# Two more tiles' skip term moved from TensorE to VectorE, with x's rows kept in the spare half of a small tile

## The chip, the cores and the metric

One Trainium2 chip, one of its cores. The time is that of one execution on the device in microseconds (us), as the median of several; lower is better. The engines are named as the profile names them: PE (TensorE, matrix products; PEld is its loading of weights), DVE (VectorE), ACT (ScalarE), POOL (GpSimd) and SP (SyncE, which here only issues transfers).

## The reference

Input x has 2048 rows (positions) of 512 channels. Two branches are computed from it and mixed by a gate per row. In the kernel's types all is bf16 outside, with sums in fp32.

```python
g = sigmoid((x * gate_w).sum(-1, keepdims=True))
# branch a: a diagonal complex recurrence over the 2048 positions, with a skip term
Bu = einsum("bld,pd->blp", x, B_bar)
for t in range(L):
    h = Lam_bar * h + Bu[:, t, :]
a = 2.0 * einsum("blp,dp->bld", hseq, Cmat).real + x * Dskip
# branch b: linear attention, 32 heads of 16; features are softmax(p) and softmax(-p)
phi_q, phi_k = features(q @ w_phi), features(k @ w_phi)
o = (phi_q @ (phi_k^T v)) / (phi_q . sum(phi_k) + 1e-6)
b = o @ wo
out = g * a + (1 - g) * b
```

The change is about `x * Dskip`, the skip term.

## The kernel before

The 2048 positions are sorted by their residue modulo 8, so that the recurrence can be run on blocks of eight positions; a tile is 128 positions of one residue, and there are 16 tiles. The output stage takes them in the order of the list `order`; "tile n" below is the n-th of that list.

**How the order of the work is set.** Each piece of work is a Python generator, `st_...`, that issues a few instructions for one engine and yields. The string `ORDER` (lines 24 to 53) lists some 850 tokens, and line 983's loop calls one generator for each. A token is a stage's name with, after `@`, the PSUM banks (of eight) that it uses, and after `:D` the wish that its copy or scaling be done by DVE rather than by ACT. The tile framework adds the semaphore waits. So the order on every engine's queue, and the choice between ACT and DVE, are written out by hand or by a planner outside the kernel; each engine works its queue strictly in order.

**The stages.** Names that matter below:

- `Z`: products of a tile of zeros with itself, the first thing on PE (line 324). The tile is `warm`.
- `Lk`, `Lx`, `Lb`, `Lc`, `Lq`, `Lv`, `Lo`, `Ld`: loads from HBM on SP's queue. `Ld` (line 260) loads the row of `Dskip` and some of x's rows.
- `k0..15`, `v0..15`, `q0..15`: products that give keys, values and queries of a tile, and their evacuation from PSUM by ACT or DVE (lines 505 to 526).
- `x`, `n`, `e`, `s` with a digit, and `X`, `N`, `E`, `S` for the four query groups of four tiles each: maximum, minimum, exponential and normalisation of the features (lines 550 to 614). `E` is two ACT instructions of 2048 elements per partition (line 567). `S` ends with a scaling on DVE (line 609) and a transpose by DMA into `phT` (line 613).
- `a0..4`: sums over the keys.
- `b`, `g`, `l`, `c`, `z`, `H`, `h`, `p`: the recurrence, with scalings by ACT (line 444) or DVE (line 446), sums on DVE and sums by POOL's DMA (line 529).
- `y`: a tile's products of the states with C (line 875); then, for a tile that is not in the list `XD`, the skip term as four products of x's transposed block with a diagonal matrix of `Dskip` (line 882), into the same PSUM bank.
- `o`: products of the query features with the key sums (line 894) into a pair of banks, logarithm and exponential on ACT (lines 898, 901), a multiplication on DVE into `on` (line 907). `O` transposes `on` by DMA (line 930).
- `t`: products with `wo`, added into y's bank (line 943), and the multiplication by the gate out of PSUM: by ACT (line 949) or DVE (line 951), or for a tile in `XD` by one DVE instruction that also adds the tile `xd` (line 947).
- `u`: for a tile in `XD`, one DVE instruction that makes `xd` = x's rows times the gate times `Dskip` (line 913).
- `R`: the store.

Before the change `XD` has tiles 8 to 11. Their x rows lie in the space of the tile `WKV` that the folded key weights leave when the last `k` stage is done; `xl` returns a tile's rows.

Of the kernel before, what the change touches and what calls it, by code (L numbers as in the profile page):

```python
# [24 lines left out]
B:D Lk Lk Z@0 Lx Z Z Z Z Z Z W00@1 Z B B B W01@2 W01 W01:D W00 W00 W10@0 Lx W11@3 Lx T0@4 B W11 T0 f1@2 Lx Lx f0@1 f0  # L25
W10:D f1:D T1@5 T1:D f2@3 f2 f3@0 f3:D k0@6 x0z:D Lx k1@7 V@3 V P U U k1 k1 k0 k0 P k3@3 P2 P P2 U P2 U k6@2 P2 P2 x0
Lx Lb Lx Lb P4 n0 P4 k3 x0 V2@6 P4 V2 P3 i3 gw P2 n0 P3 k5@7 x0 i3 x0 Lc k5 k9@3 k9 i0 Ld k2@0 M n0 i3 i3 k10@1 i3
k4@3 i0 M k2 i0 i0 i0 M Lb k10 i2 M k6 n0 k4 k7@0 k7 i2 Lb k8@7 i1 i2 x0 i1 i1 k13@6 M2 k11@0 n0 i2 k8 i1 x1 n1 x1 D
n1 x1 b200@1 i2 i1 L i0:D x1 D c1:D n1 Lc Lc i3:D n1 k11 e0 b010@7 b010 c0:D x1 n1 i2:D b200 x2 s0 c0:D s0 k12@3 k12
x2 g200@2 g200 n2 c1 b100@0 s0 b100 x2 b001@5 n2 Lv b000@7 Lc i1 b000 b111@4 b111 x2 n2 s0 n2 g000@2 b001 s0 c3:D  # L30
b011@3 b101@7 e1 x2 n2 g000 g000 Lx g001@5 g001 x3 s1 v1@4 b011 c3 s0 c2:D c2:D c1:D k14@2 g010@3 g010 Lo e2 x3 n3 s1
k13 D v0@0 v1 s1 g011@1 x3 c3:D g011 x3 g001 g011 v0 e2 k15@0 g011 g010 c0:D Lq Lq g010 s1 n3 k14 w2@6 c3 s0 D k15 n3
a0@54 s2 a0 g011 x3 n3 g011 Ld g010 g201@2 b101 Ld n3 s1 w2 g010 z0 b201@1 b201 z0 b110@7 n4 s1 x4 g101@3 g201 l2:D s2
s2 x4 n4 e3 z0 z0 w1@6 w1 b110 g100@2 g100 g101 g101 g100 s2 s2 s2 g111@1 l2:D l2:D g111 n4 g110@0 g110 e3 g110 g111
v2@2 v3@3 x4 n4 g110 g111 g111 g110 l2:D z0 v2 z0 v3 w3@2 s1 z0 g111 s3 g110 w0@7 w3 a1 a1 x4 c1 g301@6 z0 z1 z1 x4 w0
c2 g301 s3 g300@2 g300 z0 q3@7 q3 n4 e4 v5@6 z0 s2 s2 q2@2 s3 e4 q0@7 q0 z1 z1 l2:D z1 H0:D z1 s3 z1 z1 s4 v4@3 v4 q2
q1@0 H0 z1 v7@1 q1 X0 s3 q7@7 q7 z1 s4 N0 X0 v6@3 b300@0 N0 H0 b301@7 H0:D H0 N0 X0 v6 N0 s3 a2 v5 a2 c0 a2 v7 a2 X0
b301 s3 b300 q4@1 l3:D l3:D l3 c2 X0 N0 H1 H1:D H1:D q4 s4 q5@0 l3 q5 q6@7 g210@6 q6 X1 N1 h0:D H1:D E0 b211@0 X1 s4
E0 b210@7 X1 s3 b210 b311@1 b310@3 g211@2 s4 N1 S0 b211 N1 S0 s4 s4 l3:D X1 g311@7 N1 s4 g210 g210 b310 g211 g211 H1
g310@3 h0 h0 h0 g210 h1:D g211 g210 h1 b311 g211 g210 h0 g211 z2 z2 S0 z2 z2 z2 z2 g311 h1 g311 g311 h1 g310 g310 g310  # L40
S0 p00 v9@2 z2 g310 g310 g311 g311 v8@6 v15@1 S0 z2 z3 v10@7 p00 v12@3 v9 v8 S0 S0 v15 v11@6 z3 z2 z2 H2 v10 q11@2
p00:D z3 z3 z3 H2 a3 a3 H2 v12 z3 H2 H2 v11 h2 p10:D z3 z3 S0 z3 a3 a3 z3 p01 X1 h1 H3 q8@3 H3 H3 q10@6 q10 v14@7 h2
h2 H3 H3 v13@1 v13 p00:D S0 h2 q11 a4 v14 N1 q9@6 h2 q9 h3:D h3:D q12@1 a4 q8 h3 q12 X2 p10 E1 E1 a4 a4 Y S0 h3 h3 Y
X2 G q13@3 q13 G Y Y y1@1 y0@0 y0 N2 END p01 y0 o0@6 p00 p11 o0 S1 o1@4 o1 q15@2 o0 p10 p10 X2 y3@3 S0 y1 p11 S1 o0 X2
# [978 lines left out]
```

## Time and profile before

| | us |
|---|---|
| median of 3 runs | 149.02 (148.68 to 149.03) |
| the profiled execution | 148.95 |
| its span, first to last instruction | 147.2 |
| PE busy in the span | 140.8 |
| DVE busy | 135.1 |
| ACT busy | 123.4 |
| POOL busy | 45.4 |

The span is the time between the first and the last instruction of the profiled execution; what is left of its time lies around it. Busy time is the sum of the instructions' durations with overlaps counted once. Consecutive matrix products overlap in the pipeline, so a product's recorded duration is longer than the distance to the next one; distances are read from the chain or the timeline. The chain of waits starts at the last instruction and goes back at each step to what released it. In a timeline, a bracket holds the idle time in front of an instruction and what ended it. The line numbers in the rows are those of the kernel before. The granted TensorE clock was 1.00.

### The profile page before, as it was taken

The numbers are of one execution on the slowest core, as the hardware profiler recorded it, in microseconds if no ns is written. First come the engines' busy times: TensorE is split into PE (matmuls) and PEld (weight loads), VectorE is DVE, ScalarE is ACT, GpSimd is POOL, SyncE is SP. The second block draws the span as 40 slices with busy tenths as digits, with TensorE's granted clock in tenths as the row PEclk, the third lists the DMA queues.
The fourth block names the chain that finished last, engine by engine and source line by source line (L and its number), as shares of the span: only waits on it lengthen the run. The fifth ranks groups of instructions, "written<-read, shape, count | busy, mean of one in ns | idle before, by whom it ended". The sixth has DMA issues, their size and how long they took to land.

```text
span 147.2 us, 2881 instructions
## 1 busy us (share of the span) xinstructions
PE 140.8 (96%) x1014; PEld 73.3 (50%) x1014; DVE 135.1 (92%) x330; ACT 123.4 (84%) x222; POOL 45.4 (31%) x61
## 2 busy tenths in 40 slices
PE   6999999999999999999999999999979999999990
PEld 2744444444544644554454656545445554545650
DVE  2879999999999999999999999999998999979740
ACT  3479999999999999999999999999988997912110
POOL 7503600003138195797545353051003003000000
PEclk9999999999999999999999999999999999999999
DMA  5999998990846586789878969969988999999643
GB/s 123 233 184 170 181 179 160 239 290 2 195 94 90 88 114 99 80 127 169 131 111 141 144 90 191 123 126 164 208 179 153 192 214 159 199 180 271 129 111 114
DMA packets 56047, 22.63 MB, mean 154 GB/s; under 512 B 44768, under 2 KB 54880, under 8 KB 56032
## 3 DMA queue, kind: packets, MB, share of 16 engines
q1 hardware_dynamic: 47584, 15.05, 52.7%
q0 software_dynamic: 7504, 7.09, 33.8%
q10 hardware_dynamic: 944, 0.31, 0.9%
q8 instruction: 8, 0.13, 0.4%
q14 instruction: 7, 0.06, 0.1%
HBM read 2.51 MB, written 2.10 MB: 31 GB/s over the span
## 4 chain that ended last, share of the span: by engine, by line
DVE 45%; PE 36%; ACT 9%; DMA 4%; issue 3%; DVEq 0%
PE PS L875 17%; PE PS L943 8%; DVE EE L597 6%; DVE mn L544 5%; DVE mx L544 5%; DMA phT<-EE 4%; DVE EE L555 4%; DVE sq L575 4%; DVE EE L561 3%; PE PS L894 3%; PE PS L493 3%; PE PS L324 2%; DVE w L723 2%; ACT vx L137 2%; ACT Xq L137 2%
## 5 line engine op out<-in xcount | busy, mean ns | idle before, releaser
L567 ACT ACTIVATE EE<-EE 128x2048 bf16<-128x2048 bf16 x16 | 30.3, 1933 | 0.4 <-DVE EE L561 0.4
L493 PE MATMUL PS<-WKV,xT 128*128 128x480 bf16 (+1 forms) x128 | 29.2, 372 | 0.2 <-ACT WKV L137 0.2
L493 PEld LDWEIGHTS <-xT 128*128 128x128 bf16 x192 | 18.1, 97 | 19.7 <-issue 0.9
L137 ACT CAST Xq<-PS 128x480 bf16<-128x480 f32 x32 | 17.5, 592 | 0.2
L653 PE MATMUL PS<-xT,BT 128*128 128x512 bf16 x64 | 16.2, 379 | 0.0
L875 PE MATMUL PS<-C,H 128*128 128x512 bf16 x64 | 15.6, 379 | 0.0
L943 PE MATMUL PS<-Wo,oT 128*128 128x512 bf16 (+2 forms) x68 | 15.5, 366 | 0.0
L493 PE MATMUL PS<-Wq,xT 128*128 128x480 bf16 x64 | 14.9, 365 | 0.0
L641 PE MATMUL PS<-xT,BT 128*128 128x512 bf16 x64 | 14.8, 379 | 0.0
L529 POOL DMA_DIRECT2D C<-CT x4 | 6.8, 1712 | 18.1 <-DVE CT L446 18.1
L907 DVE TENSOR_TENSOR on<-PS,rd 128x512 bf16<-128x512 f32 x16 | 10.9, 684 | 1.0 <-ACT rd L901 0.9
L529 POOL DMA_DIRECT2D eb<-dg x4 | 4.8, 1201 | 22.3 <-ACT dg L444 10.9
L949 ACT ACTIVATE ot<-PS,G 128x512 bf16<-128x512 f32 (+1 forms) x10 | 6.3, 647 | 4.7 <-PE PS L943 4.7
L641 PEld LDWEIGHTS <-BT 128*128 128x128 bf16 x64 | 6.3, 98 | 7.5
L561 DVE TENSOR_TENSOR EE<-mn,Xq 128x2048 bf16<-128x2048 bf16 (+1 forms) x9 | 9.9, 1095 | 0.0
L555 DVE TENSOR_TENSOR EE<-Xq,mx 128x2048 bf16<-128x2048 bf16 (+1 forms) x9 | 9.8, 1094 | 0.0
L575 DVE TENSOR_TENSOR sq<-EE 128x2048 bf16<-128x2048 bf16 (+1 forms) x9 | 9.8, 1094 | 0.0
L943 PEld LDWEIGHTS <-oT 128*128 128x128 bf16 x68 | 6.4, 98 | 6.7
L898 ACT ACTIVATE ld<-PS 128x32 f32<-128x32 f32 x16 | 3.0, 202 | 7.8 <-PE PS L894 7.8
L597 DVE TENSOR_TENSOR EE<-EE,rc 128x2048 bf16<-128x2048 bf16 x8 | 9.6, 1210 | 0.0
L653 PEld LDWEIGHTS <-BT 128*128 128x128 bf16 x64 | 6.1, 97 | 6.9 <-issue 0.2
L137 ACT CAST vx<-PS 128x512 bf16<-128x512 f32 x16 | 9.5, 618 | 0.0
(196 smaller groups left out, 329.7 us busy)
## 6 DMA issues: line engine op xcount, KB each, us to landing
out_dram<-ot SPq DMA_DIRECT2D x7, 256.0 KB, 2.5
C<-CT POOLq DMA_DIRECT2D x4, 256.0 KB, 5.2
eb<-CT POOLq DMA_DIRECT2D x4, 256.0 KB, 4.3
eb<-dg POOLq DMA_DIRECT2D x4, 256.0 KB, 4.3
sq<-sq POOLq DMA_DIRECT2D x3, 256.0 KB, 3.8
WKV<-in_B_wqkv_dram SPq DMA_DIRECT2D x1, 512.0 KB, 4.9
Wo<-in_B_wo_dram SPq DMA_DIRECT2D x1, 512.0 KB, 4.1
WKV<-in_A_x_dram SPq DMA_DIRECT2D x2, 256.0 KB, 4.8
```

The source lines that it names most:

```text
L137: nc.scalar.copy(out=out_ap, in_=in_ap)
L493: MM(out=pt[:], lhsT=xT[:, kt, ti * P:(ti + 1) * P], rhs=W[:, kt, :], start=(kt == 0), stop=(kt == KT - 1))
L544: VT(out=dst, in0=cur[:, :, :, 0:n, :], in1=cur[:, :, :, n:2 * n, :], op=op)
L555: VT(out=half(EE, 0), in0=X5, in1=live["mx", p].to_broadcast([P, L, 8, Dh, 4]), op=ALU.subtract)
L561: VT(out=half(live["EE", p], 1), in0=live["mn", p].to_broadcast([P, L, 8, Dh, 4]), in1=X5, op=ALU.subtract)
L567: aexp(out=EE[:, l_:l_ + 2], in_=EE[:, l_:l_ + 2], func=ACT.Exp)
L575: VT(out=sq.rearrange("p q x i -> p x q i"), in0=e4[:, :, 0:2], in1=e4[:, :, 2:4], op=ALU.add)
L597: VT(out=E5[:, u:u + 2], in0=E5[:, u:u + 2], in1=rc[:, u:u + 2].to_broadcast([P, 2, 2 * NB, Dh, 4]), op=ALU.mult)
L641: MM(out=pb[:], lhsT=BT[:, ri, kt, j * P:(j + 1) * P], rhs=cells(kt, 2 * pr), start=(kt == 0), stop=(kt == KT - 1))
L653: MM(out=pgq[:], lhsT=BT[:, ri, kt, js], rhs=cells(kt, r1), start=(kt == 0), stop=(dst == 0 and j in LJ and kt == KT - 1))
L875: MM(out=py[:], lhsT=hs[j][ri], rhs=C2[:, 1 - ri, j, c:c + w], start=(j == 0 and ri == 0), stop=False)
L943: MM(out=py[:], lhsT=oT[:, g, :], rhs=Wo[:, g, c:c + w], start=False, stop=(g == HG - 1))
```

## The change

`XD` grows from tiles 8 to 11 to tiles 8 to 13. For tiles 12 and 13 the four products of line 882 are gone, there are two more `u` stages, and the last step of `t12` and `t13` (on DVE before too) adds `xd`. The x rows of the two new tiles are loaded by one more `Ld` into the tile `warm`, which becomes twice as wide: its first half holds the zeros of `Z`, and once `Z` is done the two halves take the rows of the two tiles. `ORDER` is replaced by another string with the same tokens and the new ones, so the order on all engines, the banks and the choices of `:D` differ from the first token on.

```diff
-XD = (8, 9, 10, 11)
+XD = (8, 9, 10, 11, 12, 13)
...
-    warm = const.tile([P, D], BF16, name="warm")
-    nc.vector.memset(warm[:], 0.0)
+    warm = const.tile([P, 2, D], BF16, name="warm")
+    nc.vector.memset(warm[:, 0], 0.0)
...
     def xl(n):
         k = n - XD[0]
-        return WKV[:, k // 4, k % 4, :]
+        return warm[:, k - 4, :] if k >= 4 else WKV[:, 0, k, :]
...
-            nc.sync.dma_start(out=WKV[:, k // 4, k % 4:k % 4 + w, :], in_=x_tiles[:, r, 0:w])
+            nc.sync.dma_start(out=warm[:, 0:w, :] if k >= 4 else WKV[:, 0, k:k + w, :], in_=x_tiles[:, r, 0:w])
...
-            MM(out=pz[:], lhsT=warm[:, 0:P], rhs=warm[:], start=True, stop=True)
+            MM(out=pz[:], lhsT=warm[:, 0, 0:P], rhs=warm[:, 0], start=True, stop=True)
```

Of `ORDER`, the stretches around the second and the last query group and the end, before and after:

```diff
 ORDER = """
...
-N2 q15 o1 S1 o2@6 o2 N2 o2 S1 S1 y3 N2 o1 p01 y3 p10 y2@2 S1 S1 o2 S1 O0 p30 p30 o3@4 o3 o3 y1 y2 X2 y2 q14@6 q14 N2
-y6@7 o3 y6 t1 y7@6 G E2 E2 X3 N3 t0 y6 S1 X3 N3 G t0 X3 S1 o4@4 t1 y7 y7 o5@0 o4 o4 N3 O1 t2 X3 p01 N3 S2 S2 S2 o5 o5
-t2 o4 S2 o5 S2 t3 t3 y4@4 S2 X3 S1 o6@0 S2 S2 o6 R0 o7@2 p20 y4 y4 o7 N3 p01 o6 o6 p20 o7 o7 y5@5 p30 E3 y5 O2 E3 y5
-p20 S2 y8@0 t5 t4 p30:D y11@1 S2 R1 o9@2 p20 p20 p30 y8 t4 t5 o8@4 S3 p11:D p11 S3 S3 o8 S3 y11 o8 o8 o9 o9 o9 O3 t6
...
-t10 u10 o14@2 y13 o14 o14 t10 o14 y13 y12 O6 o15@4 u11 t11 o15 o15 y15@23 y12 y15 O7 t12 t13 R5 y15 t14 o15 O8 t14
-t12:D t13:D R6 t15 t15:D t15 R7 t15 R8 R8
+N2 q15 o2 S1 N2 X2 y3 y3 S1 p10 N2 o2 o3 S1 S1 p01 p11 p30 y0 X2 N2 y1@2 y1 y1 S1 p30 p10 S1 O1 G p30 q13@4 q13
+q14@6 q14 X3 G y6@7 y6 N3 S1 S1 y7@6 X3 S1 N3 E2 X3 t0 E2 t1 t0 S2 t1 R0 N3 t2 S2 t2 p01 y6 y7 S2 y7 X3 o4@4 o4 S2
+o5@2 o5 o4 N3 o4 o5 p01 S2 t3 t3 S2 S2 o5 y4@1 y4 o7@2 o6@4 S2 p20 y4 X3 N3 p11 o6 o7 O2 o6 y5@0 o6 o7 p20 y5 o7 y5 S2
+E3 y11@4 p20 S2 t5 t4 E3 p30:D p20 p11:D y8@5 t4 t5 p30 o8@2 o8 p20 o8 S3 O3 p31:D y8 S3 S3 S2 p21 o9@0 t6 o9 o9 S3 S3
...
+o14@0 R4 y12 O6 y13 o14 t10 o14 o14 O7 t11 R5 o15@2 o15 o15 o15 O8 y14 y15@01 y15 t12 t13 u12 t14 u13 y15 t12 t13 R6
+t14 R7 t15 t15:D R8 t15 t15 R8
```

Counted over the whole string, the marks `:D` that only the order before has are two of `H1`, two of `p00`, and one each of `H0`, `W01`, `l2`, `t12` and `t13`; those that only the new order has are one each of `W00`, `l3` and `h2`. (`t12` and `t13` stay on DVE without the mark, as tiles of `XD`.)

More of the change, by code (lines that the diff above doesn't have):

```diff
@@ L24 @@
 ORDER = """
[L25 to L44, printed above, removed]
@@ L50 @@
-t9 y14@7 p21 S3 S3 O5 o12@2 p21 p21 p31 t8 S3 p21 p21 o12 o12 y12@0 t11 o12 R2 o13@2 o13 o13 u9 R3 t9 o13 R4 y14 y14
-t10 u10 o14@2 y13 o14 o14 t10 o14 y13 y12 O6 o15@4 u11 t11 o15 o15 y15@23 y12 y15 O7 t12 t13 R5 y15 t14 o15 O8 t14
-t12:D t13:D R6 t15 t15:D t15 R7 t15 R8 R8
+Z@0 Z Z Z Lk Lk Z Z Z Z W00@1 Lx Lx Lx Lx B:D W01@2 B B B W01 W00 W11@0 Lx W01 B W11 W00:D W10@3 T0@4 T0 Lb W10:D f1@2
+f0@1 f0 T1@0 f1:D Lx f2@3 T1:D f3@5 f2 f3:D k0@6 k1@7 V@3 V U P P k0 k0 U k1 P2 k1 Lc P2 P U P2 P2 U P2 k2@3 k2 n0 P4
@@ new lines @@
+v12 h1 z3 z3 z3 z3 H2 v15 z3 z3 H2 H2 z3 a3 v10 q8@0 z3 h1 H3 H3 a3 p10:D p10 a3 h2:D h2 S0 S0 S0 h2 H3 h2 q8 q9@3 a4
+H3 H3 v13 X1 N1 S0 v14@2 q10@0 a4 q9 v14 a4 a4 Y G h2 h3:D h3:D q10 h3 Y p01 Y p01 E1 Y q11@2 y2@3 y2 y3@0 q11 h3 h3
+END o0@4 E1 N2 o1@6 X2 G o0 p00 p00 S1 o1 o0 o0 X2 q12@2 o1 q12 o1 y0@1 p10 X2 y0 O0 S1 y2 p11 q15@2 o2@4 o2 o3@6 o3
+o3 N2 q15 o2 S1 N2 X2 y3 y3 S1 p10 N2 o2 o3 S1 S1 p01 p11 p30 y0 X2 N2 y1@2 y1 y1 S1 p30 p10 S1 O1 G p30 q13@4 q13
+q14@6 q14 X3 G y6@7 y6 N3 S1 S1 y7@6 X3 S1 N3 E2 X3 t0 E2 t1 t0 S2 t1 R0 N3 t2 S2 t2 p01 y6 y7 S2 y7 X3 o4@4 o4 S2
@@ new lines @@
+o5@2 o5 o4 N3 o4 o5 p01 S2 t3 t3 S2 S2 o5 y4@1 y4 o7@2 o6@4 S2 p20 y4 X3 N3 p11 o6 o7 O2 o6 y5@0 o6 o7 p20 y5 o7 y5 S2
+E3 y11@4 p20 S2 t5 t4 E3 p30:D p20 p11:D y8@5 t4 t5 p30 o8@2 o8 p20 o8 S3 O3 p31:D y8 S3 S3 S2 p21 o9@0 t6 o9 o9 S3 S3
+o8 t7 o9 y11 y10@2 t6 t7 S3 S3 p21 o10@6 p11 p21 o11@0 o10 o10 R1 y10 S3 S3 o10 y9@3 o11 o11 o11 p31 p31 O4 y14@6 u9
+p31:D p31 y9 t9 t8 y13@7 u8 t8 t9 S3 o12@0 o12 y12@5 O5 S3 R2 R3 t10 o12 o12 o13@0 o13 o13 p21 p21 t11 y14 u10 o13 u11
+o14@0 R4 y12 O6 y13 o14 t10 o14 o14 O7 t11 R5 o15@2 o15 o15 o15 O8 y14 y15@01 y15 t12 t13 u12 t14 u13 y15 t12 t13 R6
```

16 lines of the change are left out of this document (15 added, 1 removed).

## The prediction

> **What bounds the kernel now.** I read the page first, then busy time by stretches of 10 us, then the chain of waits in order of time. Two lines of the page:
>
> ```profile
> PE 140.8 (96%) x1014; PEld 73.3 (50%) x1014; DVE 135.1 (92%) x330; ACT 123.4 (84%) x222; POOL 45.4 (31%) x61
> ...
> DVE 45%; PE 36%; ACT 9%; DMA 4%; issue 3%; DVEq 0%
> ```
>
> Three engines are almost full by the first; by the second the chain that ended last runs mostly over DVE and PE. The columns of the stretches are the stretch, its length, then busy us (and instructions) of PE, PEld, DVE, ACT, POOL, the clock and the DMA share.
>
> ```profile
> 10.00:20.00 10.00, 10.00 (x50) 4.70 (x49) 9.90 (x49) 9.76 (x23) 3.64 (x10) 1.00 1.08 170
> 90.00:100.00 10.00, 9.99 (x105) 5.75 (x103) 10.00 (x26) 9.97 (x20) 2.40 (x2) 1.00 1.03 137
> 100.00:110.00 10.00, 8.94 (x73) 4.83 (x71) 9.93 (x22) 9.52 (x14) 0.00 (x0) 1.00 1.19 181
> 110.00:120.00 10.00, 10.00 (x81) 5.26 (x78) 9.44 (x18) 9.26 (x17) 1.20 (x1) 1.00 0.97 187
> 120.00:130.00 10.00, 10.00 (x71) 4.92 (x68) 9.61 (x19) 7.96 (x18) 1.20 (x1) 1.00 1.01 176
> 130.00:140.00 10.00, 10.00 (x92) 5.90 (x91) 8.00 (x13) 2.08 (x8) 0.00 (x0) 1.00 0.87 203
> ```
>
> PE is busy without a break except once, about 1 us between 100 and 110. ACT has nearly no idle time until 110 and much of it after 130. So PE sets the end, and ACT is the engine with no room in front of it. The chain names the one break and shows PE's own pace:
>
> ```profile
> 92.11 2.59 PE PS L875 x12
> 101.92 6.49 DMA phT<-EE
> 108.45 0.43 PE PS L894 x8
> 141.54 0.22 PE PS L882 x4
> 143.31 0.62 DVE ot L951
> ```
>
> Twelve 512-column products take 2.59 us, 0.216 each; four 128-column products of the skip term take 0.22, 0.054 each. From 108.45 to 143.31 the chain is PE alone: what is taken from PE there is gained, unless something else becomes late.
>
> **The skip term on PE.** Tiles 12 and 13 lose four L882 products each: 8 x 0.054 = 0.43 us less on PE, at a place where PE never waits. [...]
>
> **The skip term on DVE.** The change puts two more instructions of L913 (`u12`, `u13`) on DVE, and the last step of tiles 12 and 13 becomes the form of L947 in place of L951:
>
> ```profile
> L947 DVE SCALAR_TENSOR_TENSOR ot<-PS,G,xd 128x512 bf16<-128x512 f32 x4 | 3.0, 748 | 0.2
> L913 DVE SCALAR_TENSOR_TENSOR xd<-WKV,G,Drow 128x512 f32<-128x512 bf16 x4 | 3.0, 742 | 0.0
> L951 DVE TENSOR_SCALAR ot<-PS,G 128x512 bf16<-128x512 f32 x2 | 1.5, 750 | 1.7 <-PE PS L943 1.6
> 138.46 0.69 DVE L907 TENSOR_TENSOR on<-PS,rd 128x512 bf16<-128x512 f32 x1
> 140.71 1.61 DVE L951 TENSOR_SCALAR ot<-PS,G 128x512 bf16<-128x512 f32 x2 [1.56 <-PE PS L943]
> ```
>
> L947 and L951 cost the same (748 and 750 ns), so DVE gains 2 x 0.742 = 1.48 us of work, all of it near the end. In the new order both lie between the last `o15` step and the last step of tile 12. There DVE now stands idle 1.56 us before its last step of tile 12, as the bracket says, so they fit with 0.08 us to spare. I cost them at nothing; if that cover were missing they would cost the overhang, at most 1.48 us.
>
> **The early load.** One more 256 KB load, on SP's queue, between the other loads and long before the first transpose of features:
>
> ```profile
> WKV<-in_A_x_dram SPq DMA_DIRECT2D x2, 256.0 KB, 4.8
> ```
>
> Its target, both halves of `warm`, is free once the last `Z` at the start of the kernel is done, and its reader comes at the very end. Behind it on SP stands only that first transpose, tens of microseconds later. It costs nothing, and at most its 4.8 us landing if an early load of weights stood behind it, which the order excludes.
>
> **The new order.** The diff also replaces ORDER, so every stage moves. Most of it is a shuffle in which the work ahead of a step changes little: PE's work ahead of `o12` is the same list in both. Three things are not a shuffle.
>
> First, work passes between DVE and ACT. In the first 116 us DVE hands to ACT three 256-element scalings (one of `H0`, two of `H1`) and two 512-element ones (`p00`), and takes one 1024-element one of `h2`; the other exchanges (`W00` for `W01`, `l3` for `l2`) cancel.
>
> ```profile
> L444 ACT ACTIVATE ms<-H,dgs 128x256 bf16<-128x256 bf16 x1 | 0.6, 556 | 0.0
> L444 ACT ACTIVATE dg<-H,dgs 128x512 bf16<-128x512 bf16 x5 | 3.5, 710 | 0.0
> L444 ACT ACTIVATE m<-H,dgs 128x1024 bf16<-128x1024 bf16 x1 | 1.2, 1184 | 0.0
> L446 DVE TENSOR_SCALAR ms<-H,dgs 128x256 bf16<-128x256 bf16 x3 | 1.2, 394 | 0.0
> L446 DVE TENSOR_SCALAR dg<-H,dgs 128x512 bf16<-128x512 bf16 x3 | 1.0, 348 | 0.0
> ```
>
> Second, a 512-element scaling of `p11`, which ACT now does after `t5`, moves ahead of the exponentials `E3`. Together ACT has, ahead of `E3` and of the evacuations `t4` and `t5` behind it, 3 x 0.556 + 3 x 0.710 - 1.184 = 2.61 us more in the durations of the rows. Consecutive ACT instructions overlap: the CT scaling at 113.20 below lasts 1.14 and the next starts at 114.24, 0.10 before its end. Five more instructions by 0.10 leave 2.11 us. DVE gets rid of 3 x 0.394 + 2 x 0.348 = 1.88 us, less one 1024-element scaling.
>
> ```profile
> 103.85 3.71 ACT L567 ACTIVATE EE<-EE 128x2048 bf16<-128x2048 bf16 x2 [0.20 <-DVE EE L561]
> 108.92 0.20 ACT L898 ACTIVATE ld<-PS 128x32 f32<-128x32 f32 x1 [0.21 <-PE PS L894]
> 110.26 0.20 ACT L898 ACTIVATE ld<-PS 128x32 f32<-128x32 f32 x1 [0.18 <-PE PS L894]
> 111.12 0.69 ACT L949 ACTIVATE ot<-PS,G 128x512 bf16<-128x512 f32 x1 [0.31 <-PE PS L943]
> 113.11 0.20 ACT L898 ACTIVATE ld<-PS 128x32 f32<-128x32 f32 x1 [0.21 <-PE PS L894]
> 113.20 1.14 ACT L444 ACTIVATE CT<-H,dgs 128x1024 bf16<-128x1024 bf16 x1
> 114.24 0.19 ACT L898 ACTIVATE ld<-PS 128x32 f32<-128x32 f32 x1
> 115.78 3.70 ACT L567 ACTIVATE EE<-EE 128x2048 bf16<-128x2048 bf16 x2
> 119.38 1.26 ACT L949 ACTIVATE ot<-PS,G 128x512 bf16<-128x512 f32 x2
> 120.77 0.42 PE L894 MATMUL PS<-KVm,phT 128*128 128x68 bf16 x8
> ```
>
> This is the stretch that decides. `E3` (the L567 row at 115.78) starts without a wait: ACT itself is what it waits for. The two evacuations behind it end at 119.38 + 1.26 = 120.64, and PE's next `o` step, which writes into the banks that they free, starts at 120.77, 0.13 later. In the new order `o9` writes into the banks that `t4` and `t5` leave, with the same amount of PE work ahead of it, so an undisturbed PE would again be there at 120.77. Behind a waiting `o9` stand all of PE's later products. What ACT is late at `t5`, PE stands still.
>
> ACT's lateness is bounded from both sides. Its own waits in this stretch (0.20, 0.21, 0.18, 0.31 and 0.21 us in the brackets) are for DVE and PE; an ACT that comes later finds the inputs there. If all 1.11 us go, `t5` is 2.11 - 1.11 = 1.00 us later; if none goes, 2.11. In the other direction, ACT could win back time before 102 us, where the table of stretches leaves it 0.24 us of idle in one stretch and 0.03 in another, or inputs from a relieved DVE could come sooner; then it is late by nothing. I take 1.00, the sum of the rows with the visible idle time used up.
>
> Third, the break at 108.45. PE waits there for the transposes of the second query group:
>
> ```profile
> PE PS L894 <- DMA phT<-EE: 1.1, 1, 1.1
> phT<-EE SPq DMA_TRANSPOSE x8, 4.6
> 100.86 0.68 DVE L609 TENSOR_TENSOR EE<-EE,rho 128x1024 bf16<-128x1024 bf16 x1
> 101.46 1.22 DVE L555 TENSOR_TENSOR EE<-Xq,mx 128x2048 bf16<-128x2048 bf16 x1
> 102.60 1.21 DVE L561 TENSOR_TENSOR EE<-mn,Xq 128x2048 bf16<-128x2048 bf16 x1
> ```
>
> In the new order the scaling that feeds the first of these transposes (L609 at 100.86) stands behind the two subtractions that now follow it (1.22 and 1.21 us, starting 1.14 apart), so it is ready about 2 x 1.14 = 2.28 us later. PE's `o4` also stands later, behind eight more 512-column products and four of the skip term: 8 x 0.216 + 0.22 = 1.95 us. The break would grow by 0.33 us. With the 4.6 us of the median transpose in place of the 6.49 of the chain it would shrink by 1.89 and vanish. I take it as unchanged, since PE must in any case wait again at `o9`, and a wait in front of a later one on the same engine is not added to it.
>
> **The sum.** -0.43 (skip term on PE) + 1.00 (PE waits for `t5`) + 0 (DVE's tail, load, break) = +0.57 us. The profiled execution took 148.95 us, with a span of 147.2 and 1.75 around it; the median of the three runs is 149.02, 0.07 above. So 149.5 for an execution like the profiled one and 149.6 us as median.
>
> **The rivals.** *ACT is not late: faster.* The 1.88 us that DVE loses let every `E` start sooner, and ACT's 2.11 us are hidden in waits further ahead. For it: DVE has 45% of the chain, more than any other engine. Against it: ACT's stretches show 9.97 of 10 us busy, and `E3` waits for nothing but ACT. It gives 149.02 - 0.43 = 148.6, and with the break of 1.1 us closed too 147.5; I would say 148.3. It decides if `t5` ends by about 120.6. Chance 0.28.
>
> *The two cancel.* ACT is late by 0.43 us, near the middle between nothing and 1.00: 149.0. For it: waits of ACT before 90 us that I did not count. Chance 0.24, for everything within 0.3% (0.45 us, about what a measurement of this kernel can tell from no change).
>
> *ACT falls behind for good: slower by more.* None of the 1.11 us is won back, because the waits for `o4` and `o6` move along with the later transposes; PE waits 2.11 us at `o9`, and the features of the last query group, which follow `E3`, come later too. 149.02 - 0.43 + 2.11 = 150.7. It takes ACT's brackets to survive. Chance 0.12.
>
> *The skip term isn't moved off the path:* the removed products are replaced by a wait for `u12` and `u13` at the end. The idle 1.56 us speaks against it; it would add at most 1.48 us, 149.02 - 0.43 + 1.48 = 150.1. It lies inside the forecast's chance.
>
> **How the numbers follow.** The forecast, ACT late by about 1 us, has chance 0.36; with the worse case slower has 0.48, the cancelling case 0.24, faster 0.28. The likeliest time is 149.6. Below it the range must take in the faster case as far as the gain without the break and some of the break, 148.2; above, nearly the whole of the case with no waiting time won back, 150.6. About one in ten is left out on either side. The forecast's own range is 149.4 to 150.1.
>
> **What would show it.** In the changed kernel's groups L882 should count 40 products and L913 and L947 six each. The step is right if on ACT's timeline `E3` starts about 1 us after 115.78, the two L949 behind it end near 121.6, and PE shows an idle bracket of about 1 us in front of an L894, released by ACT. It is wrong if those L949 end by 120.7 and PE runs through; then the end should come 0.43 us sooner. If the break at L894 behind the transposes is gone from the waits and no later break has come, the faster rival is right. If DVE's last steps of tiles 12 and 13 show no idle bracket in front, the tail has become the bound.

## The result, and the profile after

The changed kernel takes 151.38 us (median of 6 runs, 150.43 to 151.8) against 148.95 us of the kernel before on the same chip: ratio 1.0149, 95% interval 1.011 to 1.0189. It is slower by 2.4 us, where 0.6 was forecast and 150.6 was the upper end of the range. The profiled execution took 151.53 us with a span of 149.7.

Busy time of the engines and the chain that ended last, by engine and by line, of the changed kernel:

```profile
PE 140.1 (94%) x993; PEld 72.1 (48%) x1006; DVE 136.2 (91%) x328; ACT 123.9 (83%) x226; POOL 45.4 (30%) x61
...
DVE 49%; PE 21%; DMA 17%; issue 4%; ACT 4%; POOL 2%; POOLq 0%; DVEq 0%
```

PE's busy time has hardly changed, but its share has fallen from 96% to 94%, and DMA's share of the chain has grown from 4% to 17%. What PE waited for (us in total, times, longest), without the waits of the first 90 us:

```profile
PE PS L894 <- DMA phT<-EE: 2.2, 2, 1.2
PE PS L943 <- DMA oT<-on: 0.6, 1, 0.6
PE PS L875 <- DVE on L907: 0.3, 1, 0.3
```

Before, one wait of 1.1 us for the transposes of features stood in this place. Now there are two long waits for them, one for the transposes of the outputs (`oT`), and none that ACT ends (the longest that ACT ends anywhere is 0.25 us, at 85 us). The chain in order of time (start, us, what) says where:

```profile
86.01 8.62 DMA phT<-EE
94.68 0.68 PE PS L894 x16
...
105.15 5.74 DMA phT<-EE
110.93 0.68 PE PS L894 x16
...
119.75 7.04 DMA phT<-EE
126.84 0.68 PE PS L894 x16
...
141.10 3.98 DMA oT<-on
145.13 0.84 PE PS L943 x4
145.99 0.62 DVE ot L951
```

PE stands still 1.20 us at `o0` (94.68), 0.12 at `o4`, 1.00 at `o10` (126.84) and 0.58 at the last tile's `t15` (145.13). A simple ledger turns this into a sum. Take for each step on PE its start less 0.422 ns (216 ns / 512) for each column of all products ahead of it in the program; what is left is the lag that PE has gathered up to there, in us:

| PE's step | lag before | lag after | what the after kernel lost more since the row above |
|---|---|---|---|
| last of `a4` (about 90) | 7.33 | 7.73 | 0.40 |
| `o1` (95) | 7.63 | 9.25 | 1.22 |
| `o4` (108 / 111) | 9.11 | 9.65 | -1.08 |
| `t4` (118 / 119) | 9.24 | 10.44 | 0.66 |
| `o11` (126 / 127) | 9.32 | 11.68 | 1.16 |
| `t15` (142 / 145) | 9.48 | 12.58 | 0.74 |

That is 3.10 us more lag, less the 0.43 us of the eight removed products: 2.67 us later at `t15`, of which the tail behind it gives 0.2 back. The rows of the three waits for transposes carry 3.1 of it, the one that the kernel before had (at `o4`) and the new one hasn't takes 1.1 off, 0.66 us are lost around `y11`, in part behind DVE's L907 (0.28 at 117.2), and 0.40 us had been lost ahead of `a4`, which nothing here traces to a cause.

**Why the transposes land later.** Part 3 of both pages lists a queue that the prediction did not look at:

```profile
q8 instruction: 8, 0.13, 0.4%
```

Eight packets of 16 KB. That they are blocks of program is read from the queue's name and from what moves them; below, one is called a fetch of code. In before they start at 18.0, 40.9, 59.2, 77.0, 93.0, 106.4, 123.4 and 138.9 us, 126 PE products apart on average (100 weight loads begun at the first, 984 at the last, 101 to 159 between neighbours); in after the last four start at 92.6, 107.2, 124.2 and 141.5. They go with the count of PE's products: in seven traces, of before and of the six runs below that keep its order but for a few tokens and leave the products of zeros whole, the last four start when PE has begun 631 to 634, 730 to 733, 858 to 860 and 984 to 986 of its weight loads, the last of them at times up to 1.9 us apart. (A second such queue, q14, has seven packets of 8 KB. One of them, at 139.72 us in the run `before_z8` below, falls into the last `oT` transposes, which take 2.41 us there; no cost of it is seen.) Here is the DMA traffic of before from 104 to 110 us (40 slices of 0.15 us; busy share of the engines, then GB/s), with the fetch of 106.4 us in it:

```profile
DMA  9999999999999999999000000006999999999999
GB/s 217 200 218 217 218 217 218 217 217 215 181 183 209 226 239 297 184 55 32 0 0 0 7 9 10 10 10 150 290 292 272 283 297 283 294 290 290 292 292 283
...
q8 instruction: 1, 0.02, 1.0%
```

From 106.6 us the rate falls from about 220 GB/s to between 0 and 10, and it resumes at 108.05. The packet of the block itself ended at 107.32. That is no more than one engine of the sixteen would move (an estimate: 220 / 16 = 14 GB/s); that an engine held by the block makes the hole, as theory C below has it, no view shows. The first half of the second group's `phT` transposes lands right behind this hole, at 108.41, and PE waits for it at `o4` (1.06 us), the only long wait of the kernel before. After, from 123 to 129 us, with the fetch of 124.2:

```profile
DMA  9999999999999999999788899939000009999999
GB/s 213 213 246 195 143 150 171 137 307 205 246 212 205 212 218 225 253 219 225 208 179 167 160 203 125 85 67 38 14 14 21 22 17 184 283 295 270 292 285 154
```

A like hole from 126.6 to 128.0, behind the end of the packet at 125.75, and in it the end of the transposes for `o10`. Here one share of sixteen comes late: fifteen of their sixteen shares had landed by 124.88, the last one landed at 126.79.

No wait of PE is a fetch's own: behind the first 5 us neither trace has a wait of PE of over 0.1 us without another releaser. The cost shows elsewhere, in the transposes that a fetch falls into (that of 106.4 us: 6.49 us with it, 4.7 to 5.1 in three runs without).

### The profile page after: what moved, and what is told of

Read it like the earlier page. It is cut to its first block, busy times and chain, and to the rows that moved or that the text cites. A ratio compares the mean times of both kernels' runs of the same rounds, so it can differ in the third digit from the quotient of the medians.

```text
span 149.7 us, 2864 instructions
## 1 busy us (share of the span) xinstructions
PE 140.1 (94%) x993; PEld 72.1 (48%) x1006; DVE 136.2 (91%) x328; ACT 123.9 (83%) x226; POOL 45.4 (30%) x61
## 4 chain that ended last, share of the span: by engine, by line
DVE 49%; PE 21%; DMA 17%; issue 4%; ACT 4%; POOL 2%; POOLq 0%; DVEq 0%
DMA phT<-EE 14%; PE PS L875 10%; DVE mn L544 6%; DVE mx L544 5%; DVE EE L597 5%; DVE EE L561 5%; DVE EE L555 4%; DVE sq L575 4%; PE PS L943 3%; PE PS L493 3%; DMA oT<-on 3%; PE PS L894 2%; DVE w L723 2%; DVE CT L446 1%; DVE dg L437 1%
## 5 line engine op out<-in xcount | busy, mean ns | idle before, releaser
L653 PE MATMUL PS<-xT,BT 128*128 128x512 bf16 x64 | 16.1, 379 | 0.1
L943 PE MATMUL PS<-Wo,oT 128*128 128x512 bf16 (+2 forms) x65 | 15.2, 366 | 0.8 <-DMA oT<-on 0.6
L641 PE MATMUL PS<-xT,BT 128*128 128x512 bf16 x64 | 15.7, 379 | 0.0
L875 PE MATMUL PS<-C,H 128*128 128x512 bf16 x61 | 14.8, 379 | 0.2
L907 DVE TENSOR_TENSOR on<-PS,rd 128x512 bf16<-128x512 f32 x16 | 10.7, 686 | 2.7 <-ACT rd L901 2.6
L529 POOL DMA_DIRECT2D eb<-dg x4 | 4.8, 1188 | 22.1 <-ACT ld L898 8.8
L949 ACT ACTIVATE ot<-PS,G 128x512 bf16<-128x512 f32 (+1 forms) x10 | 6.0, 646 | 5.2 <-PE PS L943 5.2
L529 POOL DMA_DIRECT2D sq<-sq x3 | 2.7, 902 | 25.0 <-DVE mn L544 21.8
L943 PEld LDWEIGHTS <-oT 128*128 128x128 bf16 x68 | 6.1, 98 | 7.5 <-DMA oT<-on 1.3
L444 ACT ACTIVATE dg<-H,dgs 128x512 bf16<-128x512 bf16 (+1 forms) x11 | 9.6, 874 | 0.0
```

The source lines that it names most:

```text
L641: MM(out=pb[:], lhsT=BT[:, ri, kt, j * P:(j + 1) * P], rhs=cells(kt, 2 * pr), start=(kt == 0), stop=(kt == KT - 1))
L653: MM(out=pgq[:], lhsT=BT[:, ri, kt, js], rhs=cells(kt, r1), start=(kt == 0), stop=(dst == 0 and j in LJ and kt == KT - 1))
L875: MM(out=py[:], lhsT=hs[j][ri], rhs=C2[:, 1 - ri, j, c:c + w], start=(j == 0 and ri == 0), stop=False)
L943: MM(out=py[:], lhsT=oT[:, g, :], rhs=Wo[:, g, c:c + w], start=False, stop=(g == HG - 1))
```

## The experiments

Three theories were put to the test. A: ScalarE (ACT) is late at the third exponential and at `t5`, as forecast. B: the new order puts consumers too close behind the transposes, or other traffic beside them. C: the fetches of code decide, since any change in the products ahead of them moves them against the transposes. In the kernels `skip_only` and `order_only` line numbers are two lower, in `before_z8` and `after_z8` one higher, than in the others. Ratios are to the kernel before, on the same chip.

| run | us | ratio, 95% interval |
|---|---|---|
| skip_only | 149.89 | 1.0056, 1.0037 to 1.0074 |
| order_only | 151.75 | 1.0177, 1.015 to 1.0205 |
| before_z8 | 150.79 | 1.0096, 1.0062 to 1.013 |
| after_z8 | 150.56 | 1.0113, 1.0087 to 1.0138 |
| before_z7 | 150.94 | 1.0107, 1.0067 to 1.0147 |
| skip_z7 | 151.26 | 1.0143, 1.01 to 1.0187 |
| after_z10 | 150.04 | 1.0052, 1.003 to 1.0074 |
| after_r5 | 151.19 | 1.0116, 1.007 to 1.0163 |
| after_r1 | 151.58 | 1.0161, 1.0118 to 1.0204 |
| after_all | 149.27 | 1.0018, 0.999 to 1.0046 |
| skip_r5 | 149.13 | 0.9992, 0.9968 to 1.0016 |
| skip_fix | 148.29 | 0.995, 0.9929 to 0.997 |
| before_fix | 148.39 | 0.9956, 0.9938 to 0.9975 |
| skip_fix_b | 148.21 | 0.9951, 0.9932 to 0.9971 |
| skip_fix_ot | 148.16 | 0.993, 0.9909 to 0.9951 |

### The two parts of the change apart

`skip_only` has the changed code with the order of before, edited as little as it takes:

```diff
-XD = (8, 9, 10, 11)
+XD = (8, 9, 10, 11, 12, 13)
...
-g010 g201@2 b101 Ld n3 s1
+g010 g201@2 b101 Ld Ld n3 s1
...
-o14 t10 o14 y13 y12 O6 o15@4
+o14 t10 o14 y12 O6 o15@4
...
-o15 o15 y15@23 y12 y15 O7 t12
+o15 o15 y15@23 y15 O7 t12
...
-y15 t14 o15 O8 t14 t12:D
+y15 t14 o15 u12 u13 O8 t14 t12:D
```

> The order of before, with the skip term of tiles 12 and 13 on VectorE too (x's rows in the tile of zeros, two multiplications more on VectorE behind the last L907, eight L882 products fewer), and nothing else moved. Three theories of the 2.4 us that the change lost. A, that of the prediction: ScalarE comes late to the third exponential and to t5 in the new order; here the order is the old one, so 0.43 us is won: 148.5 us. B, the new order puts the consumers too close behind the transposes: likewise 148.5 us. C, code fetches: the 16 KB blocks of the 'instruction' queue, one for each 126 or so TensorE products, each hold back one DMA engine and with it the transposes queued there by 1 to 1.5 us, and what they hit depends on how many products lie ahead of them. Here the last fetch (138.86 us in before) comes after 4 to 8 products fewer, so 0.4 to 0.8 us later against the last oT transposes (139.18 to 142.14), while TensorE wants them 0.4 us sooner: a wait of 0.3 to 1 us at the last L943 group takes back what the products gave: 148.7 to 149.5 us.

`order_only` has the order of after with tiles 12 and 13 back on PE:

```diff
-XD = (8, 9, 10, 11, 12, 13)
+XD = (8, 9, 10, 11)
...
-Lq s1 x3 Ld s1 b110 c1
+Lq s1 x3 s1 b110 c1
...
-o14@0 R4 y12 O6 y13 o14 t10
+o14@0 R4 y12 y12 O6 y13 y13 o14 t10
...
-y15 t12 t13 u12 t14 u13 y15 t12 t13 R6 t14 R7
+y15 t12 t13 t14 y15 t12:D t13:D R6 t14 R7
```

> The new order with the skip term of tiles 12 and 13 back on TensorE (eight L882 products behind the last L875 of y12 and of y13, no u12 and u13, one load fewer). All three theories put the loss into the new order, so 151.4 plus the 0.43 us of the products: 151.6 to 152.0 us, with the L894 waits for the phT transposes of 1.2 us at o0 and 1.0 us at o10 as in after. If it were the two multiplications of VectorE or the load that cost, it would be 149 us. C adds that the last fetch comes 4 to 8 products sooner than in after, which may take away the wait of 0.6 us at the last L943 group.

Measured: 149.89 and 151.75 us. The order carries the loss, as all theories had it. In `order_only` the wait at `t15` is gone, as C added; one of 0.88 us at `t2` has come instead, where the `oT` transposes with the fetch of 106.7 in them take 7.43 us (5.70 in after). But the skip term alone, which A and B put at 148.5, is slower too, with the wait at `t15` that C named, though by more than C's range (up to 149.5). PE's waits in `skip_only` (L941 is L943 of the other kernels) and the tail of its timeline:

```profile
PE PS L892 <- DMA phT<-EE: 0.9, 2, 0.6
PE PS L941 <- DMA oT<-on: 0.8, 1, 0.8
...
139.24 1.40 DVE L911 SCALAR_TENSOR_TENSOR xd<-warm,G,Drow 128x512 f32<-128x512 bf16 x2
143.26 1.05 PE L941 MATMUL PS<-Wo,oT 128*128 128x384 bf16 x8 [0.76 <-DMA oT<-on]
```

The last fetch, at 138.9 us in before, comes at 139.6 because eight products ahead of it are gone, and now falls into the last `oT` transposes, which take 3.87 us instead of 2.96. PE's `t12` starts at 139.53, 0.12 us sooner than in before, its `t15` at 143.26, 0.80 later. The two multiplications on DVE end at 140.64 and hold up nobody. That only 0.12 of the 0.43 us was left at `t12` has another reason, given under the last experiments: PE was 0.49 us late by the end of `a4` already.

### Moving the fetches

Each of the eight products of zeros at the start becomes several short ones; the columns stay the same (seven and ten leave out a few), and nothing else is edited. Eight pieces put 56 products more ahead of everything, seven 48 and ten 72:

```diff
-            MM(out=pz[:], lhsT=warm[:, 0:P], rhs=warm[:], start=True, stop=True)
+            for c in range(8): MM(out=pz[:, c * 64:(c + 1) * 64], lhsT=warm[:, 0:P], rhs=warm[:, c * 64:(c + 1) * 64], start=True, stop=True)
```

> Before, with each of the eight products of zeros at the start cut into eight of 64 columns: the same columns, 56 products more ahead of everything, in a stretch where TensorE waits for loads. By A and B nothing changes but at most 0.2 us at the start: 148.9 to 149.2 us, and the wait of 1.1 us for phT at o4 stays. By C each code fetch moves 56 products ahead in the work: that of 106.4 us, which stands in the first half of the second group's phT transposes (landing at 108.41, TensorE there at 107.4), comes at about 98.5, and the wait of 1.1 us goes or falls below 0.4: 148.0 to 148.4 us.

> After, with the same cut of the eight products of zeros (56 products more at the start). By A and B no change: 151.4 to 151.7 us, and the L894 waits for phT of 1.2 us at o0 and 1.0 us at o10 and the 0.6 us for oT at the last L943 stay. By C the fetches of 124.2 and 141.5 us move to about 115 and 135.5 us: the phT transposes of the third group's second half take 4.6 us instead of 7.0 and the last oT transposes 3.0 instead of 4.0, the waits at o10 and at t15 go, and 1.0 + 0.6 us less 0.2 us at the start are won: 149.8 to 150.3 us. The wait at o0 stays (its fetch moves from 92.6 to about 87.5, still in the same transposes).

> Before, with each of the eight products of zeros at the start as seven of 64 columns: 48 products more ahead of everything. By C (the code fetches decide) the last four fetches come at about 89, 99.3, 116 and 134 us. At 99.3 no phT transposes are in flight, so the wait of 1.1 us at o4 goes; at 116 the oT transposes of tiles 4 and 5 are nearly done (116.65 in before) and the phT transposes behind them have 0.9 us to spare: at most 0.3 us of wait for oT at t5, where the cut into eight (fetch at 115.05) waited 0.8. 148.0 to 148.5 us. By A and B, for which the fetches are incidental: 149.0 to 149.3 us, or as the cut into eight, 150.8.

> The skip term of tiles 12 and 13 on VectorE in the order of before, with the same cut into seven (48 products more at the start). By C the wait of 0.8 us that the skip term brought at the last L943 group, where the fetch of 139.6 us stood, goes with the fetch (now at about 134), and the wait at o4 too: 0.4 us below the run without the skip term and with the same cut, 147.5 to 148.1 us. If the wait at t15 came from the multiplications u12 and u13 on VectorE or from TensorE arriving sooner, it stays, and the time is that of the cut without the skip term or 0.3 us over it.

> After, with each of the eight products of zeros as ten of 50 columns: 72 products more at the start, 0 to 0.5 us there. By C the last four fetches come at about 85, 97.5, 112.7 and 133.5 us, all between transposes: the waits at o0 (1.2 us), o10 (1.0) and t15 (0.6) of after go, and those of the cut into eight at y7 (0.9), t5 (1.3) and y11 (0.5, against 0.3 in after) do too: 148.6 to 149.6 us. By A (ScalarE late at the third exponential and t5) or B (the consumers too near): 150.5 to 151.7 us, with waits for phT or behind ScalarE left wherever the fetches are.

The times of after moved as C said, though by less than forecast (150.56 and 150.04, down by 0.8 and 1.3 us). Those of before and `skip_z7` went the other way, up by 1.3 to 1.8 us: `before_z8` missed the ranges of all three theories, `before_z7` missed C's and came near the 150.8 that was left to A and B, and `skip_z7` came out 0.3 above `before_z7`, a time that was left to the multiplications on DVE or an early PE, but without the wait at `t15` that belonged to it. The traces say why, in part. In `before_z8` (its trace is of an execution of 149.45 us, 1.3 below the median, so most of the loss lies outside it) the fetch of 106.4 is at 99.0, the transposes take 4.8 us (6.49 before), and the wait at `o4` is gone, as expected. But the next fetch, at 115.0, now falls into the `oT` transposes of tiles 4 and 5, and the first, at 8.6, into the loads at the start (times of the two waits in us, then the landing of those transposes):

```profile
PE PS L944 <- DMA oT<-on: 0.8, 1, 0.8
PE PS L494 <- DMA xT<-in_A_x_dram: 0.7, 1, 0.7
...
phT<-EE SPq DMA_TRANSPOSE x1, 4.8
```

In `after_z8` the three waits of after are gone and three others stand in their place, one for the same `oT` transposes (fetch at 116.0), one behind ACT, one behind DVE:

```profile
PE PS L944 <- DMA oT<-on: 1.3, 1, 1.3
PE PS L876 <- ACT Xq L137: 0.9, 1, 0.9
PE PS L876 <- DVE on L908: 0.5, 1, 0.5
```

In `after_z10` the three waits of after are gone as well, and PE waits behind ACT (1.3 us at 67 us), for the same `oT` transposes (1.0, fetch at 115.6) and behind DVE (0.5) instead. `before_z7` and `skip_z7` missed in the same way: the fetches expected at 116 came at 117.3 and 115.8, in those `oT` transposes again, and PE waited 1.1 and 1.6 us at `t5`. Transposes are not all that a fetch can hit: in both, the fetch of 68.5 and 68.3 us stands in three of GpSimd's sums (L529), which take 5.9 to 6.6 us against 4.9 to 5.7 in before, and through a later sum and DVE PE waits 0.9 and 0.7 us at 79 us. So, as far as these runs go, moving the fetches only chooses what they hit. What the shifts do give is each transfer with and without a fetch, over all runs, from issue to landing in us:

| transfer, order | with a fetch in it | without |
|---|---|---|
| `phT`, second group, first half, before | 6.49, 6.36, 6.51, 6.53, 6.19, 6.51, 6.48 | 4.81, 5.14, 4.74 |
| `oT` of tiles 4 and 5, before | 5.44, 6.36, 6.31 | 5.03, 4.16, 4.26, 5.09, 4.88, 5.03, 5.12 |
| `phT`, first group, first half, after | 8.62, 8.51, 8.46, 8.47, 8.56 | 7.36 |
| `phT`, third group, second half, after, R1 in place | 7.04, 7.19, 6.79 | 6.43, 5.80 |
| last `oT`, store R5 ahead of it, both | 3.98, 3.87, 4.06 | 2.41 to 2.66 |

By the means of the rows a fetch costs the transfer 1.2 to 1.5 us, and 0.9 in the fourth. Where it came right at the issue it cost less (7.36 us in the third row in `after_z8`; 2.96 and 2.89 in the last row in before and `order_only`), and so it did near the end (the fourth row's counterpart in the order of before: 4.5 to 4.7 us with a fetch in its last 0.7 us, 4.3 to 4.4 without). The fourth transfer takes longer even without a fetch than the 4.3 to 4.7 us of its counterpart in the order of before: that is B's share.

### Traffic beside the transposes

Two stores stand beside late transposes in after: R5 on SP's queue ahead of the last `oT`, and R1 (121.74 us) within those for `o10`. Each was moved alone:

```diff
-o14 O7 t11 R5 o15@2 o15 o15 o15 O8 y14 y15@01 y15
+o14 O7 t11 o15@2 o15 o15 o15 O8 R5 y14 y15@01 y15
```

> After, with one move: the store of tiles 10 and 11 (R5) is issued behind the last oT transposes instead of ahead of them, on SyncE's queue. In after the fetch of 141.5 us held back one engine's share of that store to 144.56, and the transposes behind it landed at 145.08. By C with the order on the queue as its amplifier the transposes no longer stand behind the delayed share, land about 143.5 to 144.5, and the wait of 0.6 us at the last L943 group goes: 150.7 to 150.9 us. If the fetch holds the transposes themselves back as much, or if the wait comes from TensorE being early, it stays: 151.3 to 151.5 us. The waits at o0 and o10 stay in either case.

```diff
-o11@0 o10 o10 R1 y10 S3 S3
+o11@0 o10 o10 y10 S3 S3
...
-p31 p31 O4 y14@6 u9 p31:D
+p31 p31 O4 R1 y14@6 u9 p31:D
```

> After, with one move: the store of tiles 2 and 3 (R1, issued at 121.74 us in after, in the middle of the third group's second phT transposes) is issued behind O4. Those transposes took 7.0 us with a fetch in them and 5.8 to 6.4 without one, against 4.3 to 4.6 in the order of before. By B (traffic that the order puts beside the transposes: this store, and GpSimd's transfer of 120.38) they come down by 0.5 to 1.5 us and the wait of 1.0 us at o10 falls to 0 to 0.4: 150.4 to 150.9 us. By C alone, the fetch being in them still, they stay near 7 us and so does the wait: 151.2 to 151.5 us.

With R5 behind them the last transposes, which still have a fetch beside them (141.8), take 3.18 us instead of 3.98, and the wait at `t15` is gone from the trace: shown. The time, 151.19 us, cannot tell it: its interval overlaps that of after. (It was not one engine's share of the store that came late in after: twelve of the sixteen shares of R5 landed between 144.38 and 144.56.) With R1 moved the transposes for `o10`, with their fetch, still take 6.57 us, and PE's wait there falls from 1.00 to 0.61: the store alone is not the cause there. The time (151.58) cannot tell, since in this trace a fetch at 106.3 made the `oT` transposes ahead of `t2` take 7.29 us and PE wait 0.74 for them. Without the fetch and with the store they took 6.43 and 5.80; where both are away (next run) 4.42.

### Treating the waits

`after_all` has both moves and fills the wait at `o0` with `q12`, which needs none of what `o0` waits for:

```diff
-h3 h3 END o0@4 E1 N2
+h3 h3 END q12@2 o0@4 E1 N2
...
-o0 o0 X2 q12@2 o1 q12 o1
+o0 o0 X2 o1 q12 o1
...
-o11@0 o10 o10 R1 y10 S3 S3
+o11@0 o10 o10 y10 S3 S3
...
-p31 p31 O4 y14@6 u9 p31:D
+p31 p31 O4 R1 y14@6 u9 p31:D
...
-o14 O7 t11 R5 o15@2 o15 o15 o15 O8 y14 y15@01 y15
+o14 O7 t11 o15@2 o15 o15 o15 O8 R5 y14 y15@01 y15
```

> After, with the three waits for transposes treated: the products of q12 (0.8 us) ahead of o0, R1 behind O4, R5 behind O8. If these waits are the loss of the change, 0.8 + 0.6 + 0.6 to 1.0 us are won and it comes to 149.0 to 149.6 us, with the waits behind VectorE's L907 near 117 us (0.3 to 0.7) left. If the loss lies in ScalarE's or VectorE's lateness and the waits only show it, TensorE loses elsewhere what it wins here: 150.5 to 151.4 us.

149.27 us: 2.1 of the 2.4 us are back. The twelve runs lie between 148.35 and 150.33; the trace is of one of 148.82. PE's waits behind DMA and DVE in it:

```profile
PE PS L894 <- DMA phT<-EE: 0.3, 1, 0.3
PE PS L875 <- DVE on L907: 0.3, 1, 0.3
PE PS L943 <- DMA oT<-on: 0.2, 1, 0.2
...
119.81 1.24 ACT L949 ACTIVATE ot<-PS,G 128x512 bf16<-128x512 f32 x2
121.31 0.42 PE L894 MATMUL PS<-KVm,phT 128*128 128x68 bf16 x8
```

In this trace PE lost nowhere else what it won: the waits were the loss, and A finds no support. ACT ends `t4` and `t5` at 121.05, and PE reaches the `o` step that writes where they stood at 121.31.

The same for `skip_only`: first R5 behind the last transposes,

```diff
-O7 t12 t13 R5 y15 t14 o15 u12 u13 O8 t14 t12:D t13:D
+O7 t12 t13 y15 t14 o15 u12 u13 O8 R5 t14 t12:D t13:D
```

> The skip term of tiles 12 and 13 on VectorE in the order of before, and the store of tiles 10 and 11 (R5) issued behind the last oT transposes instead of ahead of them. By C the store's share that the fetch of 139.6 us held back no longer stands ahead of the transposes, the wait of 0.8 us at the last L943 group falls below 0.2, and what remains of the change's own worth is seen: 149.0 to 149.3 us, against 149.9 with R5 ahead and 149.0 to 149.2 without the skip term on VectorE. If u12 and u13 on VectorE make that wait, it stays: 149.7 to 150.0 us.

then work that is ready put ahead of `o4` and of `t5`:

```diff
-t0 X3 S1 o4@4 t1 y7 y7 o5@0 o4 o4
+t0 X3 S1 y7 y7 o4@4 t1 o5@0 o4 o4
...
-p20 S2 y8@0 t5 t4 p30:D y11@1 S2 R1 o9@2
+p20 S2 y8@0 y11@1 t5 t4 p30:D S2 R1 o9@2
```

> As the run before, and TensorE given other work where it waits for the second group's phT transposes: the last two steps of y7 (12 products, 1.1 us) go ahead of o4, and the first step of y11 (four products, 0.9 us) ahead of t5, so that the oT transposes of tiles 4 and 5 have time. By C (the waits are for transposes and can be covered) the wait at o4 goes and TensorE is 0.6 to 1.1 us earlier there; ScalarE, which ends t4 and t5 behind the third exponential near 120.6 us, gives back what TensorE is too early at o8: 148.2 to 149.0 us. By A (ScalarE bounds this stretch) all of it is given back at o8: 149.0 to 149.3 us.

149.13 and 148.29 us, both as C expected. In `skip_fix` the page of PE's waits holds nothing but the start and one short wait:

```profile
PE PS L324 <- DVE warm L156: 1.2, 1, 1.2
PE PS L493 <- ACT WKV L137: 0.3, 1, 0.3
PE PS L627 <- DVE EE L597: 0.2, 1, 0.2
```

Its second group's transposes take 6.53 us, fetch and all; PE has other work meanwhile. At 0.995 of the kernel before (0.9929 to 0.997) it is faster than both kernels.

### What the skip term is worth by itself

`before_fix` has the moves of `skip_r5` and `skip_fix` and keeps the skip term on PE; `skip_fix_b` is `skip_fix` again, on the same chip.

```diff
-t0 X3 S1 o4@4 t1 y7 y7 o5@0 o4 o4
+t0 X3 S1 y7 y7 o4@4 t1 o5@0 o4 o4
...
-p20 S2 y8@0 t5 t4 p30:D y11@1 S2 R1 o9@2
+p20 S2 y8@0 y11@1 t5 t4 p30:D S2 R1 o9@2
...
-O7 t12 t13 R5 y15 t14 o15 O8 t14 t12:D t13:D
+O7 t12 t13 y15 t14 o15 O8 R5 t14 t12:D t13:D
```

> Before, with the three moves of order alone (the last two steps of y7 ahead of o4, the first step of y11 ahead of t5, R5 behind O8) and the skip term of tiles 12 and 13 left on TensorE. The prediction's first step put the skip term at 0.43 us of TensorE, at a place where it never waits. If that is right, this kernel is 0.3 to 0.5 us slower than the same with the skip term on VectorE: 148.6 to 148.8 us where that has 148.3. If the skip term is worth nothing where no transfer is disturbed, the two agree within 0.1 us; if VectorE's two multiplications cost more than the products gave, this one is faster.

> The same three moves with the skip term of tiles 12 and 13 on VectorE, as in the run of the call before (148.29 us), taken again on the same chip as its counterpart without the skip term: 148.1 to 148.5 us, 0.3 to 0.5 below the counterpart by the prediction's first step.

148.39 and 148.21 us: the moves alone bring 0.6 us, and what the skip term adds, 0.2 us where 0.3 to 0.5 was expected, is within the intervals. In `skip_fix` the last step on DVE waits for the store that the moves put later (its output goes into the buffer that R5 empties), and in `before_fix` it does not, so that wait was taken away too:

```profile
143.33 0.62 DVE L951 TENSOR_SCALAR ot<-PS,G 128x384 bf16<-128x384 f32 x1 [1.44 <-DMA out_dram<-ot]
```

```diff
-            live["ot", g_] = pools["op"][1].tile([P, 2, D], BF16, name="ot")
+            live["ot", g_] = warm if n == NTI - 1 else pools["op"][1].tile([P, 2, D], BF16, name="ot")
```

> The skip term on VectorE with the three moves, and one more edit: the last tile's output is written into the tile of zeros, whose rows of x have been used by then, and not into the buffer that the store R5 empties. With the three moves, the store R5 behind the last oT transposes landed at 143.23 us, and the last L951 (143.33), which writes into that buffer, waited for it: TensorE was done about 0.5 us before. In the counterpart with the skip term on TensorE the last L951 waited for TensorE alone. If that wait hides the skip term's 0.43 us, it comes out now: 147.6 to 147.9 us, against 148.2 to 148.3 without the edit and 148.4 for the counterpart. If the skip term is worth nothing in itself, 148.1 to 148.4.

The step then starts at 142.80, behind PE, but the time is 148.16 us, not 147.6 to 147.9: the wait had hardly set the end, and the time lies in the range that was named for a skip term worth nothing. In the traces PE needs 48.6 us from the third step of `a4` to `t12` in `before_fix` and 48.2 us in `skip_fix_b` and `skip_fix_ot`, 0.45 less, as the prediction's first step has it. But these two traces are 0.7 us behind at that `a4`, from later first loads and from short waits of 0.1 to 0.2 us each between 58 and 72 us. By ratios the skip term is worth between nothing and 0.4 us.

The short waits come in part from the load that the skip term brings. In the order of before the x rows of tiles 12 and 13 are still arriving (issued at 37.2 to 37.7 us, landed at 42.3 to 43.8) when GpSimd's sum `sq` is issued at about 40, and a fetch comes between 40.7 and 41.9 us:

| sum `sq` issued at about 40 us | issue to landing, us |
|---|---|
| load and fetch in it (`skip_only`, `skip_r5`, `skip_fix`, `skip_fix_b`, `skip_fix_ot`) | 4.61, 4.57, 4.58, 4.53, 4.38 |
| load alone (`skip_z7`) | 3.73 |
| fetch alone (`before`, `before_fix`) | 3.77, 3.55 |
| neither (`before_z7`, `before_z8`) | 3.46, 3.33 |

In the first four of the first row DVE waits for this sum (0.05 to 0.13 us, L583). Against before it falls back by 0.13 to 0.20 us there, and by another 0.28 to 0.35 behind a scaling that takes 0.62 to 0.69 us instead of 0.34, for a reason that no view shows. ACT's exponentials follow, and PE loses 0.3 us between 50 and 63 us. So a part of the 0.43 us goes back here. Whether another place for the load keeps it was not tried.

## Why the prediction was right and wrong

**Skip term on PE, -0.43 us.** Right as a term (0.45 in the traces), L882 counts 40 products as forecast, but it brought a price with it: eight products fewer shift the last code fetch into the last transposes. In the old order that turned a lead of 0.12 us at `t12` into a lag of 0.80 at `t15` (`skip_only`), and in the new order the wait at `t15` is there with the skip term on DVE (0.58) and not without it (`order_only`).

**DVE's tail and the load, nothing.** Right in the new order: from 35 us to `o0` PE's steps in after and in `order_only`, which has no third load, keep their distance within 0.1 us. In the old order the load was not free (see above); the prediction looked for what stands behind it on SP's queue alone, and not at GpSimd's transfers beside it. The groups of after, then the end of DVE's timeline, where the two L913 from `warm` run in a gap:

```profile
L947 DVE SCALAR_TENSOR_TENSOR ot<-PS,G,xd 128x512 bf16<-128x512 f32 x6 | 4.4, 748 | 1.3 <-PE PS L943 1.2
L882 PE MATMUL PS<-Dd,xT 128*128 128x128 bf16 x40 | 3.7, 219 | 0.0
L913 DVE SCALAR_TENSOR_TENSOR xd<-warm,G,Drow 128x512 f32<-128x512 bf16 x2 | 1.4, 746 | 0.0
...
140.99 1.41 DVE L913 SCALAR_TENSOR_TENSOR xd<-warm,G,Drow 128x512 f32<-128x512 bf16 x2
142.64 1.62 DVE L947 SCALAR_TENSOR_TENSOR ot<-PS,G,xd 128x512 bf16<-128x512 f32 x2 [0.24 <-PE PS L943]
```

**ACT late by 1.00 us at `t5`, and PE waiting for it: the step that failed.** In after the lateness looks as forecast: the third exponentials start 0.87 us later than in before, and the two L949 end at 121.49, where 121.6 was named. That is partly luck, since PE was late itself. In `after_all`, where PE has hardly any of its waits left, the exponentials start at 116.21 and the two L949 end at 121.05, 0.43 and 0.41 us later than in before. The sum of rows left out two stretches in which ACT of before has room, 0.32 us idle from 40 to 50 us and 0.35 from 70 to 80.

```profile
116.65 3.69 ACT L567 ACTIVATE EE<-EE 128x2048 bf16<-128x2048 bf16 x2
120.25 1.24 ACT L949 ACTIVATE ot<-PS,G 128x512 bf16<-128x512 f32 x2
...
120.85 0.42 PE L894 MATMUL PS<-KVm,phT 128*128 128x68 bf16 x8
121.97 0.42 PE L894 MATMUL PS<-KVm,phT 128*128 128x68 bf16 x8
```

But `o9` starts at 121.97, behind them, without a bracket. The forecast had "an undisturbed PE" there at 120.77, and PE was not undisturbed: at `t4` it stood 1.2 us further behind than before. Even PE without most of those waits (`after_all`) meets no wait behind L949. The term of 1.00 us was 0.

**The break at `o4` "as unchanged".** Wrong. It had been a transpose with a code fetch in it (6.2 to 6.5 us against 4.7 to 5.1 without one), not a transpose of that length; the prediction saw the 6.49 us beside the median of 4.6 and did not ask what made the difference. In after the wait at `o4` is 0.12 us.

**"Most of it is a shuffle".** Here lies the rest. The prediction looked for what becomes later in front of PE's consumers at two places and took the order elsewhere as neutral, a term put at nothing that measured 3.1 us of lag at three transposes. Ahead of `o0`, for one, before has the `y1` and `y0` products between the last `a4` and `o0`, and its transposes land 1.9 us before PE gets there (92.88, 94.76); in after PE is there at 93.47 and the transposes at 94.63. Of that the fetch makes about 1.2 us (8.5 us on average with it, 7.36 without), as long as the wait itself. No rival named a transfer that becomes later at `o0`, `o10` and `t15`, and these three make the miss.

## What to carry to other kernels

Where a kernel keeps one engine busy to the last microsecond, list for each of its waits on a transfer the spare time, issue and landing included, in both orders: a change that moves nothing but the order spends that spare time. A transfer that takes 1 to 2 us longer than its like deserves a look at the DMA rate in narrow slices; here a hole in which the rate fell from about 220 GB/s to between 0 and 10 went with a code fetch, and the fetch moved when the number of products ahead of it changed (from 106.4 to 99.0 us with 56 more, in `before_z8`). Put work that is ready ahead of such a wait, and stores behind the transposes on a shared queue: on this kernel that was worth 0.6 us without any change of the arithmetic.
